# Gated linear attention and an MLP-mixer on one core: float32 warming products, constants from three engines, one relu per row tile of batch 0, and a new order for all engines

## The chip, the cores and the metric

The kernel runs on one core of a Trainium2 chip. The metric is the device time of one execution in microseconds (us); lower is better. Engines are named as the profile names them: PE (TensorE, matrix products), PEld (its weight loads), DVE (VectorE), ACT (ScalarE), POOL (GpSimd) and SP (SyncE, which only issues transfers here). A page of the profile shows one execution.

## The reference, cut to what matters

```python
# q, k, v, f_logit: (4, 8, 768, 48), float32
f = 1.0 / (1.0 + np.exp(-f_logit))
for t in range(S):                      # 768 steps, state (B, H, 48, 48)
    state = f[:, :, t, :, None] * state + np.einsum('bhd,bhe->bhde', k[:, :, t], v[:, :, t])
    y[:, :, t] = np.einsum('bhd,bhde->bhe', q[:, :, t], state)
x = y as (B, S, H * D)                  # (4, 768, 384)
xt = x.transpose(0, 2, 1)
h = np.maximum(xt @ w_tok1, 0.0) @ w_tok2       # (768 x 256), (256 x 768)
u = x + h.transpose(0, 2, 1)
h2 = np.maximum(u @ w_ch1, 0.0) @ w_ch2         # (384 x 1536), (1536 x 384)
return u + h2
```

## The kernel before, in words

Each of the four batches goes through two stages. The attention stage cuts the 768 steps into six chunks of 128. For a chunk it takes the logarithms of the gates (`exp`, `ln` on ACT), the low half of their split into two bf16 numbers (`lo`, a subtraction on DVE or POOL), their running sums as matrix products with a triangle of ones (`sums` on PE), the two factors `G` and `Gi` (exponentials on ACT), the gated q and k (`gated`, DVE), their transposes (`turn` on PE, `turned` the copy out of PSUM), the scores within the chunk (`scores`, PE), their causal mask (`masked`, DVE), and the result `y` from scores and v and from the carried state. The state is carried by `tsum` (state plus k'v, DVE), `state` (times the chunk's decay, DVE), and two `spread` copies into the bf16 operand `state_bd` of the next chunk's `y`. Batch 0 handles its chunks in three pairs, and there `within` is the product of masked scores and v for both chunks, and `parts` the k'v products. `x_bf` and `x_nat` are copies of `y` in bf16 and in float32.

The mixer stage of a batch is `tok1` (12 products of 384 columns into two row tiles), `h1T` (the relu of each row tile), `tok2` (12 products), `u` and `u_bf` (the sums with x), `ut`/`uT` (transposes), `ch1` (24 tiles of three products), `zT` (their relus), `ch2` (six tiles of twelve products), the last sum and the store. In batch 0 each `h1T` row tile is relued in two halves of 192 columns.

Nothing is scheduled by a program at run time. Each engine runs its queue in order and waits at semaphores. The order is the string `ORDER`: each number is one operation in the order in which the code made it, a letter behind it names the engine (A, D or G for ACT, DVE or POOL) where it can choose, and numbers behind colons are PSUM banks. A token z or s is a run of products whose result is not used, 512 or 64 columns wide, on a tile of ones (`steady`, made by a DVE memset); they keep PE at work where it would wait. POOL also issues nearly all loads, each holding its queue for about 0.9 us; loads rotate over eight semaphores, so that one waits for the landing of the load eight places ahead of it. The loads of f for batch 0 and all stores go through SP.

Constants (zeros around the 48 used columns of 64, the triangle `tri`, the identity, pair masks `pmask0`, `pmask1`, `inc2`, `exc2`) are made once, by DVE except for `tri`, which POOL makes from a tile that DVE has zeroed. `L870` is the line of the idle products, `L698` the masks of batch 0, `L536` those of the others, `L730` and `L549` the state's decay, `L352` and `L354` the relus on ACT and DVE.

## Time and profile before

| | |
|---|---|
| median of three timed runs | 173.82 us (173.77 to 174.5) |
| profiled execution, first to last instruction | 172.8 us |
| PE busy, share of the span | 95%, clock 0.999 of full |
| DVE, ACT, POOL busy | 75%, 64%, 45% |
| queue of POOL's loads | 13.77 MB, 91.7% of the span on 16 DMA engines |

The profiled execution has no time of its own beside its span. The median of the runs lies 1.0 us above that span; that is what is around the first and last instruction. A busy share of PE says little on how full it is, since products overlap in the records; how close together they start says more, and so does the chain of waits.

### The profile page before, as it was taken

The numbers are of one execution on the slowest core, as the hardware profiler recorded it, in microseconds if no ns is written. First come the engines' busy times: TensorE is split into PE (matmuls) and PEld (weight loads), VectorE is DVE, ScalarE is ACT, GpSimd is POOL, SyncE is SP. The second block draws the span as 40 slices with busy tenths as digits, with TensorE's granted clock in tenths as the row PEclk, the third lists the DMA queues.
The fourth block names the chain that finished last, engine by engine and source line by source line (L and its number), as shares of the span: only waits on it lengthen the run. The fifth ranks groups of instructions, "written<-read, shape, count | busy, mean of one in ns | idle before, by whom it ended". The sixth has DMA issues, their size and how long they took to land.

```text
span 172.8 us, 4455 instructions
## 1 busy us (share of the span) xinstructions
PE 164.4 (95%) x1758; PEld 103.6 (60%) x1762; DVE 129.1 (75%) x287; ACT 109.7 (64%) x246; POOL 78.0 (45%) x102
## 2 busy tenths in 40 slices
PE   6889998999999999999999999999999999999991
PEld 2465755566676666676667566666565656656660
DVE  6989996978997789989969859887786355581132
ACT  3997938999893656799999685479933430444100
POOL 2999846998566893799663330010101012000000
PEclk9999999999999999999999999999999999999999
DMA  5999999999997998999999995638155006250054
GB/s 146 217 169 175 246 210 210 157 122 129 197 134 154 182 109 197 133 60 114 108 135 69 63 141 135 144 81 157 32 154 154 1 19 163 89 188 0 2 200 168
DMA packets 89573, 22.74 MB, mean 132 GB/s; under 512 B 82288, under 2 KB 88736, under 8 KB 89552
## 3 DMA queue, kind: packets, MB, share of 16 engines
q0 software_dynamic: 69600, 13.77, 91.7%
q1 hardware_dynamic: 19952, 8.69, 19.6%
q8 instruction: 14, 0.23, 0.6%
q14 instruction: 7, 0.06, 0.1%
HBM read 25.17 MB, written 4.72 MB: 173 GB/s over the span
## 4 chain that ended last, share of the span: by engine, by line
PE 75%; ACT 8%; DVE 5%; issue 1%; DVEq 0%
PE ps L838 26%; PE ps L819 23%; PE ps L750 4%; PE ps L766 4%; PE ps L408 3%; ACT zT L352 2%; PE ps L495 2%; PE ps L456 2%; PE ps L560 2%; PE ps L457 1%; ACT L L367 1%; PE ps L870 1%; PE ps L424 1%; PE ps L804 1%; PE ps L556 1%
## 5 line engine op out<-in xcount | busy, mean ns | idle before, releaser
L838 PE MATMUL ps<-w_ch,zT 128*128 128x384 bf16 (+2 forms) x300 | 52.9, 319 | 0.0
L819 PE MATMUL ps<-uT,w_ch 128*128 128x384 bf16 x288 | 52.4, 326 | 0.3 <-ACT GG L468 0.2
L352 ACT ACTIVATE zT<-ps 128x384 bf16<-128x384 f32 x61 | 28.2, 493 | 19.6 <-PE ps L819 14.6
L838 PEld LDWEIGHTS <-zT 128*128 128x128 bf16 x300 | 28.4, 98 | 17.4 <-issue 0.2
L819 PEld LDWEIGHTS <-w_ch 128*128 128x128 bf16 x288 | 26.9, 97 | 17.0 <-issue 0.7
L354 DVE TENSOR_SCALAR zT<-ps 128x384 bf16<-128x384 f32 x35 | 18.9, 554 | 10.4 <-PE ps L819 8.9
L536 DVE TENSOR_TENSOR AmT<-ps,tri_bf 128x512 bf16<-128x512 f32 x36 | 23.1, 683 | 2.3 <-PE ps L408 2.1
L348 POOL CAST state_bd<-state 48x192 bf16<-48x192 f32 x24 | 9.0, 376 | 34.6 <-DVE state L549 22.2
L844 DVE TENSOR_TENSOR x_nat<-x_nat,ps 128x384 f32<-128x384 f32 (+2 forms) x25 | 12.8, 534 | 10.3 <-PE ps L838 9.8
L264 POOL DMA_DIRECT2D qk_sb<-in_q_dram x16 | 15.9, 1000 | 0.8 <-issue 0.8
L264 POOL DMA_DIRECT2D qk_sb<-in_k_dram x16 | 15.7, 983 | 0.3 <-issue 0.3
L264 POOL DMA_DIRECT2D v_sb<-in_v_dram x16 | 15.7, 983 | 0.1
L782 DVE TENSOR_TENSOR x_nat<-x_nat,ps 128x384 f32<-128x384 f32 x21 | 10.8, 549 | 4.2 <-PE ps L766 4.1
L750 PE MATMUL ps<-x_bf,w_tok 128*128 128x384 bf16 x48 | 13.2, 326 | 0.3 <-DVE zT L698 0.2
L348 POOL CAST u_bf<-x_nat 128x384 bf16<-128x384 f32 x6 | 3.0, 506 | 20.7 <-DVE x_nat L782 20.7
L374 POOL TENSOR_TENSOR Llo<-L 128x384 bf16<-128x384 f32 x10 | 8.2, 826 | 6.4 <-ACT L L367 6.3
L485 DVE TENSOR_TENSOR qk<-qk_sb,GG 128x768 bf16<-128x768 bf16 x18 | 9.9, 555 | 1.4 <-ACT GG L468 1.4
L870 PE MATMUL ps<-x_nat 128*128 128x512 bf16 x26 | 8.7, 460 | 2.0 <-DVE x_nat L279 1.5
L466 ACT ACTIVATE GG<-ps 128x384 bf16<-128x384 f32 x18 | 8.7, 492 | 2.5 <-PE ps L457 2.3
L344 ACT ACTIVATE x_bf<-ps 128x384 bf16<-128x384 f32 x13 | 6.5, 499 | 5.9 <-PE ps L560 5.0
L766 PE MATMUL ps<-h1T,w_tok 128*128 128x384 bf16 x48 | 9.4, 326 | 0.8 <-ACT h1T L352 0.6
L468 ACT ACTIVATE GG<-ps 128x384 bf16<-128x384 f32 x18 | 8.9, 492 | 1.8 <-PE ps L457 1.6
(96 smaller groups left out, 266.4 us busy)
## 6 DMA issues: line engine op xcount, KB each, us to landing
out_dram<-x_nat SPq DMA_DIRECT2D x23, 192.0 KB, 2.2
f_sb<-in_f_logit_dram POOLq DMA_DIRECT2D x3, 1152.0 KB, 11.1
f_sb<-in_f_logit_dram SPq DMA_DIRECT2D x3, 384.0 KB, 4.2
w_ch<-in_moe_w_ch_dram POOLq DMA_DIRECT2D x2, 576.0 KB, 13.2
qk_sb<-in_q_dram POOLq DMA_DIRECT2D x12, 96.0 KB, 6.6
qk_sb<-in_k_dram POOLq DMA_DIRECT2D x12, 96.0 KB, 5.6
v_sb<-in_v_dram POOLq DMA_DIRECT2D x12, 96.0 KB, 4.5
w_ch<-in_moe_w_ch_dram POOLq DMA_DIRECT2D x1, 1152.0 KB, 10.0
```

The source lines that it names most:

```text
L264: lambda eng=eng, into=into, of=of: eng.dma_start(out=into, in_=of),
L348: nc.gpsimd.tensor_copy(out_, in_)
L352: nc.scalar.activation(out_, in_, AF.Relu, bias=0.0, scale=1.0)
L354: nc.vector.tensor_scalar(out_, in_, 0.0, None, ALU.max)
L536: add(("masked", b, c, p), DVE, lambda half=half, made=made: nc.vector.tensor_tensor(half, made(), tb4, ALU.mult), need=["tri_bf"], make=[ ...
L750: add(("tok1", b, rt, kt), PE, lambda rt=rt, kt=kt, pm=pm: nc.tensor.matmul(banks[pm.at][:, 0:DM], lhsT=w_tok1[:, kt, rt * 128:(rt + 1) * ...
L766: nc.tensor.matmul(banks[pm.at][:, 0:DM], lhsT=w_tok2[:, kt, tt * 128:(tt + 1) * 128], rhs=h1T[:, kt, :], start=(kt == 0 and not held), st ...
L782: nc.vector.tensor_tensor(to, un, banks[pm.at][:, 0:DM], ALU.add)
L819: nc.tensor.matmul(banks[pm.at][:, 0:384].rearrange("p (n t) -> p n t", t=128), lhsT=w[:, kt, c0:c0 + 128], rhs=uT[:, rows3, kt, :], start ...
L838: nc.tensor.matmul(banks[pm.at][:, 0:n1 - n0], lhsT=zT[:, kt, tt * 128:(tt + 1) * 128], rhs=w_ch2[:, kt, n0:n1], start=(kt == 0), stop=(kt ...
L844: add(("sum", b, tt, n0), DVE, lambda un=un, pm=pm, n=n1 - n0: nc.vector.tensor_tensor(un, un, banks[pm.at][:, 0:n], ALU.add), make=[("x_n ...
L870: nc.tensor.matmul(banks[NBANK - 1][0:rows, 0:cols], lhsT=steady[:, 0:rows], rhs=steady[:, 0:cols], start=True, stop=True)
```

## The change

Five things are changed at once.

- Idle products: the tokens z and s of before (13 of 512 columns at the start, then 17 more up to the end of batch 0's attention) give way to tokens w: one float32 product of the given number of columns on the same tile of ones, read as float32. There are three of 512 columns and eleven bf16 products of 64 columns at the start, and one of 512 and one of 128 columns ahead of the second `within`.
- Constants: memsets may stand on DVE or POOL, copies on DVE or ACT. The new list puts eleven memsets on POOL and five copies on ACT.
- State: the decay product may stand on POOL; twelve of its sixteen products from the second chunk on do so, three of them in batch 0.
- `h1T` of batch 0 is relued in whole rows of 384 columns: two operations in place of four.
- `ORDER` is a new list: order, engines and banks of all operations. Counts by engine that change most: `zT` on ACT 61 to 55, on DVE 35 to 41; `lo` on POOL 11 to 15, on DVE 13 to 9; `u_bf` on ACT 14 to 11, on POOL 6 to 10; `turned` on ACT 8 to 5, on DVE 10 to 13; `uT` on ACT 5 to 2, on DVE 7 to 10; `x_bf` and `x_nat` on ACT 25 to 29, on DVE 20 to 16.

```diff
+HALVES = False
+STATES = (DVE, POOL,)
 ORDER = """
-32 33 10 5 34 15 21 9 8 22 13 11 0 1 36 24 27 2 49 3 6 35 12 14 20 23 25 26 50 28 7 37 51 52D 54 53D 38 17 z13 105:0
+w512 w512 w512 s11 32 0G 6G 33 8G 20D 9D 5G 34 13D 7G 1 21G 35 2 24A 23A 27D 3A 37 26A 29D 14D 28 49 17D 36 19D 51 22G
...
     def memset(name, tl, value, make, own):
-        once(name, DVE, lambda: nc.vector.memset(tl, value), make, own)
+        op = once(name, (DVE, POOL), None, make, own)
+        op.fn = lambda: (nc.gpsimd if op.engine == POOL else nc.vector).memset(tl, value)
+
+    def copied(name, out_, in_, make, own, need):
+        op = once(name, (DVE, ACT), None, make, own, need)
+        op.fn = lambda: copy_on(op.engine, out_, in_)
...
-                add(("state", b, c), DVE, lambda: nc.vector.tensor_tensor(state, tsum, gb, ALU.mult),
-                    need=["tsum", ("glast", g4)], make=["state"], kind=small)
+                decayed(b, c, gb, ("glast", g4))
...
+    def decayed(b, c, gb, key):
+        op = add(("state", b, c), STATES, None, need=["tsum", key], make=["state"], kind=("el", HP * D, True, 1))
+        op.fn = lambda: (nc.gpsimd if op.engine == POOL else nc.vector).tensor_tensor(state, tsum, gb, ALU.mult)
...
-            half = DM // 2 if b == 0 else DM
+            half = DM // 2 if b == 0 and HALVES else DM
...
     def idle(n, cols):
+        if not cols:
+            wide = spare[:, 0:512].bitcast(FP32)
+            nc.tensor.matmul(banks[NBANK - 1].rearrange("p (a n) -> p a n", n=128)[:, 0:n // 128], lhsT=wide[:, 0:128],
+                             rhs=wide[:, 0:128].unsqueeze(1).broadcast_to((128, n // 128, 128)), start=True, stop=True)
+            return
```

**PE, around the second `within`.** Before, PE's queue holds one last product of `within` (L711), then six idle products (one is shown), then the past-state product of chunk 2 (L736):

```order
L711 LDWEIGHTS zT
L711 MATMUL ps_114<-v_sb_72,zT 128x48
L870 LDWEIGHTS x_nat_101
L870 MATMUL ps_119<-x_nat_101 128x512
L736 LDWEIGHTS zT
L736 MATMUL ps_112<-state_bd_98,zT 128x96
```

With the change the two float32 idle products stand ahead of `within` (now L719), behind the last scores (L676):

```order
L676 LDWEIGHTS zT
L676 MATMUL ps_114<-zT 64x128
L877 MATMUL ps_119<-x_nat_101 128x512
L877 MATMUL ps_119<-x_nat_101 128x128
L719 LDWEIGHTS zT
L719 MATMUL ps_116<-v_sb_72,zT 128x48
```

Nothing idle is left between `within` and the products with the state.

**DVE, at the end of batch 0's attention.** Before, from the last mask on (L698; `x_bf` is L346, the halves of `h1T` L354):

```order
L698 TENSOR_TENSOR zT<-ps_117,x_nat_101 128x512
L728 TENSOR_TENSOR tsum<-state,ps_116 128x192
L730 TENSOR_TENSOR state<-tsum,gpair_120 128x192
L346 CAST x_bf_102<-ps_114 128x384
L346 CAST x_bf_102<-ps_117 128x384
L346 CAST x_bf_102<-ps_113 128x384
L354 TENSOR_SCALAR h1T<-ps_115 128x192
L354 TENSOR_SCALAR h1T<-ps_118 128x192
L346 COPY x_nat_99<-ps_112 128x384
```

With the change (masks are L706, `tsum` L736, `state` L577, copies L279, `h1T` L359):

```order
L706 TENSOR_TENSOR zT<-ps_115,x_nat_101 128x512
L736 TENSOR_TENSOR tsum<-state,ps_114 128x192
L577 TENSOR_TENSOR state<-tsum,gpair_120 128x192
L279 CAST x_bf_102<-ps_116 128x384
L279 CAST x_bf_102<-ps_117 128x384
L279 CAST x_bf_102<-ps_113 128x384
L359 TENSOR_SCALAR h1T<-ps_114 128x384
L279 COPY x_nat_99<-ps_116 128x384
```

One whole row of `h1T` stands in the place of two halves; the other row is one ACT operation.

**POOL, in the second half of batch 0's attention.** Before, from the second token weights on (`spread` is L348, loads of q, k, v L264, of weights L270):

```order
L270 DMA w_tok_65<-in_moe_w_tok_dram 128x2x768 [waits DMASW3_49]
L348 CAST state_bd_98<-state 48x4x48
L270 DMA w_ch_67<-in_moe_w_ch_dram 128x3x768 [waits DMASW4_49]
L270 DMA w_ch_66<-in_moe_w_ch_dram 128x3x768 [waits DMASW5_49]
L348 CAST state_bd_97<-state 48x4x48 [waits DVE_49,PE_49]
L264 DMA qk_sb_70<-in_q_dram 128x8x48 [waits DMASW6_49]
```

With the change (`state` is L577, `spread` L281, loads L266 and L272, `lo` L379):

```order
L272 DMA w_tok_65<-in_moe_w_tok_dram 128x2x768 [waits DMASW3_49]
L577 TENSOR_TENSOR state<-tsum,gpair_120 128x192 [waits DVE_49,Activation_49]
L266 DMA qk_sb_70<-in_q_dram 128x8x48 [waits DMASW4_49]
L266 DMA qk_sb_70<-in_k_dram 128x8x48 [waits DMASW5_49]
L272 DMA w_ch_67<-in_moe_w_ch_dram 128x3x768 [waits DMASW6_49]
L281 CAST state_bd_98<-state 48x4x48 [waits Pool_49]
L577 TENSOR_TENSOR state<-tsum,gpair_121 128x192 [waits DVE_49,Activation_49,Pool_49]
L266 DMA qk_sb_70<-in_k_dram 128x8x48 [waits DMASW7_49]
L281 CAST state_bd_97<-state 48x4x48 [waits PE_49,Pool_49]
L266 DMA qk_sb_70<-in_q_dram 128x8x48 [waits DMASW0_49]
L272 DMA w_ch_66<-in_moe_w_ch_dram 128x3x768 [waits DMASW1_49]
L577 TENSOR_TENSOR state<-tsum,gpair_121 128x192 [waits DVE_49,Activation_49,Pool_49]
```

The state's products now stand in the queue that issues the loads, behind loads that wait for landings of earlier ones.

119 lines of the change are left out of this document (58 added, 61 removed).

## The prediction

> **What bounds the kernel now.** I read the page's first part and the table of windows, then the chain of waits, then the timeline of the first 34 us and the groups by line.
>
> ```profile
> span 172.8 us, 4455 instructions
> 10.00:20.00 10.00, 8.91 (x219) 6.22 (x218) 9.58 (x27) 8.14 (x19) 9.01 (x12) 1.00 1.81 196
> 20.00:30.00 10.00, 8.92 (x185) 5.58 (x180) 8.09 (x16) 6.62 (x16) 6.03 (x10) 1.00 1.10 213
> 33.90:51.80 17.90, 17.80 (x201) 11.69 (x201) 16.29 (x34) 16.87 (x41) 13.90 (x18) 1.00 1.97 145
> 72.60:105.10 32.50, 32.22 (x357) 21.24 (x355) 26.78 (x56) 28.15 (x65) 19.10 (x21) 1.00 1.69 105
> 145.76 10.72 PE ps L819 x66
> ```
>
> A window's row gives its length, then busy us of PE, PEld, DVE, ACT, POOL, and the granted clock. The last row is a piece of the chain: 66 products in 10.72 us, 0.162 us each, PE without a gap. From 138 us to the last product the chain is such pieces, so the end is moved only by what happens earlier. From 33.9 to 105 us DVE and ACT are nearly as full as PE (16.29 and 16.87 of 17.9 us), and PE sometimes waits for them. From 10 to 20 us DVE is the full one (9.58 of 10 us); PE is then kept going by idle products. The first 34 us are the costly part: the chain there runs so:
>
> ```profile
> 24.68 1.24 PE ps L870 x5
> 26.73 0.51 PE ps L711 x32
> 29.21 0.37 DVE h1T L354
> 29.61 0.56 ACT h1T L352 x2
> 30.19 0.37 DVE h1T L354
> 30.60 1.46 PE ps L766 x8
> 33.19 0.34 PE ps L804 x6
> 33.88 0.26 PE ps L819
> 47.47 0.45 PE ps L495 x8
> 82.60 0.51 ACT zT L352
> ```
>
> At 24.68 us PE runs its own idle products (1.24 us) while the state's product, `parts` and the other `within` stand behind them. At 29.21 us four half relus follow one another before `tok2` (L766) can go on at 30.60. At 33.88 the chain reaches the channel products (L819), whose first stands at 33.81. A transpose takes 0.056 us (L804 and L495, 6 and 8 of them). At 82.60 the chain lies on ACT.
>
> **The change part by part.** *The start.* These rows carry it:
>
> ```profile
> 1.46 4.72 PE L870 MATMUL ps<-x_nat 128*128 128x512 bf16 x13 [1.46 <-DVE x_nat L279]
> 3.32 0.29 POOL L282 TENSOR_SCALAR_AFFINE_SELECT tri_bf<-tri_bf 128x128 bf16<-128x128 bf16 x1 [2.88 <-DVE tri_bf L277]
> 5.94 0.96 DVE L396 TENSOR_TENSOR Llo<-L 128x384 bf16<-128x384 f32 x2
> 8.33 1.00 ACT L622 ACTIVATE GG<-ps 128x384 bf16<-128x384 f32 x2
> 9.88 1.17 DVE L629 TENSOR_TENSOR qk<-qk_sb,GG 128x384 bf16<-128x384 bf16 x4 [0.64 <-DMA qk_sb<-in_k_dram]
> 24.07 1.88 DVE L698 TENSOR_TENSOR zT<-ps,x_nat 128x512 bf16<-128x512 f32 x3
> 27.26 1.54 DVE L346 CAST x_bf<-ps 128x384 bf16<-128x384 f32 x3
> L277 DVE MEMSET L<- 128x256 f32 x3 | 0.8, 272 | 0.0
> L348 POOL CAST state_bd<-state 48x192 bf16<-48x192 f32 x24 | 9.0, 376 | 34.6 <-DVE state L549 22.2 <-DVE state L544 6.1 <-PE ps L736 3.1
> L549 DVE TENSOR_TENSOR state<-tsum,glast 128x192 f32<-128x192 f32 x12 | 4.2, 351 | 0.8 <-ACT state_bd L344 0.6 <-POOL state_bd L348 0.2
> L346 DVE COPY qkT<-ps 128x1024 bf16<-128x1024 bf16 x9 | 6.2, 686 | 0.4 <-PE ps L495 0.4
> L383 ACT ACTIVATE L<-f_sb 128x768 f32<-128x768 f32 x2 | 1.7, 854 | 0.0
> ```
>
> POOL waited 2.88 us for DVE's zeros; now it makes them, and four larger memsets, itself. No row shows a POOL memset of that size: between DVE's 0.27 and POOL's cast of 192 columns scaled to 256 (0.376 x 256/192 = 0.5), the four take 1.1 to 2.0 us, and the triangle is there between 2.0 us and 3.3 us; I take 2.8, nearer the cast, and the first load then issues 0.6 us earlier. That load is now k's, not q's, so the 0.64 us that DVE waited for k at 9.88 go. `Gi` of the first pair still starts at 8.33, since ACT has the same exponentials and logarithms before it; the list puts the earlier-needed one first. DVE's gated products can start at about 8.9 instead of 9.88.
>
> From there to the last mask (24.07 + 1.88 = 25.95 us) DVE's work hardly changes: three states go (3 x 0.35) and two small constants (about 0.6); a `lo` (0.48), an `x_bf` (0.51) and a `turned` (0.69) come: about zero. But ACT now has a logarithm of 0.85 us ahead of the second `Gi` and two more `spread` copies, and DVE waits for it about 1 us in all at the second and fourth gated products and at chunk 5's. I keep the last mask at 25.9. Gain so far 0, bounds -0.5 and +1.
>
> *The idle products.* The 1.24 us at 24.68 are gone from behind `within`. What is late next is the last mask: the second `within`, at 26.73 before, can run at 26.0, and `tsum`, which waited for `parts` behind those idle products, runs right behind the mask. The new idle products stand ahead of the first of the two `within`, whose masks end near 24.4, and the scores end near 22: no trace shows a float32 product; between the price of a bf16 one (1.24/5 = 0.25 us for 512 columns) and four times that the two take 0.3 to 1.2 us, inside that wait. At the start three of them take 1.1 us (at 4.72/13 = 0.36 us each) to 4.4 us; the `sums` wait for `lo` until 6.7 us (6.9 before, 5.94 + 0.96), so neither end delays them.
>
> *The end of batch 0's attention.* Last mask 25.9; `tsum` and `state` 0.7 us: 26.6; `spread` 0.36 on two engines: 27.0; chunk 5's `y` behind chunk 4's, one `sums` and three `tok1`: 27.5 to 27.8; its `x_bf` 0.51: 28.3, against 28.8 before (27.26 + 1.54). Row 0's relu on DVE (0.5, priced like that cast) runs beside the last three `tok1` of row 1; row 1's on ACT (0.5, as the `Gi` above) ends at 29.6 to 29.8. `tok2` gets both rows then; before, at 30.60. The first channel product follows from the same `u`, `ut`, `uT` steps at 33.0 instead of 33.81: 0.8 us. By then PE has also done one more chunk's `sums` (two products, 0.32), eight transposes of batch 1 (0.45) and one more `ut` (0.17), all placed where it waited: 0.95 us less to do later. The lead is 1.75 us; I take 1.6, bounds 0 (masks late) and 2.2.
>
> *The rest.* Rows for what changes engine:
>
> ```profile
> L374 POOL TENSOR_TENSOR Llo<-L 128x384 bf16<-128x384 f32 x10 | 8.2, 826 | 6.4 <-ACT L L367 6.3
> L374 DVE TENSOR_TENSOR Llo<-L 128x384 bf16<-128x384 f32 x8 | 4.4, 561 | 0.0
> L352 ACT ACTIVATE zT<-ps 128x384 bf16<-128x384 f32 x61 | 28.2, 493 | 19.6 <-PE ps L819 14.6 <-issue 4.3 <-ACT grow L472 0.2
> L344 ACT ACTIVATE u_bf<-x_nat 128x384 bf16<-128x384 f32 x12 | 6.1, 522 | 6.0 <-DVE x_nat L782 6.0
> L344 ACT ACTIVATE qkT<-ps 128x1024 bf16<-128x1024 bf16 x3 | 3.1, 1022 | 0.0
> ```
>
> From the first channel product on, DVE loses nine states (3.2 us), five `lo` (2.8) and five copies of `y` (2.6) and gains six `zT` (3.1, priced like those copies) and two `turned` (1.4): -4.1 us (three `uT` come, and some single operations of that size go). ACT loses six `zT` (3.0), five `u_bf` (2.6), two `turned` (2.0), two `uT` (1.0, priced like `zT`) and five gate operations now done earlier (2.5), and gains five copies of `y` (2.5) and two logarithm steps (1.0): about -8 us. POOL takes nine states, six `lo` (5.0) and four `u_bf` (2.0) and has four loads fewer. A POOL state is priced by the two `lo` rows: 0.351 x 826/561 = 0.52 us; bounds 0.35 and 0.83. So 12 us leave the two engines that crowd PE; in the two later windows quoted they were busy 88 us together. What PE then waits for is partly not load but order, which the new list also draws anew: I take a gain of 0.5 us, bounds -1.5 and +2.
>
> One row speaks against the moves: beside POOL's subtraction a small DVE copy took 0.78 us, without it 0.20.
>
> ```profile
> 9.04 0.20 DVE L323 COPY x_nat<-x_nat 64x64 bf16<-64x64 bf16 x1
> 10.97 0.83 POOL L396 TENSOR_TENSOR Llo<-L 128x384 bf16<-128x384 f32 x1 [0.23 <-ACT L L383]
> 11.07 0.78 DVE L323 COPY x_nat<-x_nat 64x64 bf16<-64x64 bf16 x1
> ```
>
> The Trainium skill, Advanced Engine Details and Errata, Mode Summary, says the same: the second SBUF port of the Vector engine is shared with GPSIMD, and two-port Vector instructions and GPSIMD instructions block each other. By that rule every such DVE instruction beside the new POOL work would stretch, and the sum would lose its 0.5 us. I keep the term: one instruction is no rate, and copies within SBUF are few after the start.
>
> The sum is made against the profiled execution: 172.8 - 1.6 - 0.5 = 170.7 us, and the 1.0 us by which the runs' median lies above its span: **171.7 us**.
>
> **The rivals.** *POOL's queue holds the state back (slower).* The place is the third state of batch 0 on POOL. It stands behind two loads that wait for the landings of f of batch 1 and of v's last piece, which follows f:
>
> ```profile
> f_sb<-in_f_logit_dram POOLq DMA_DIRECT2D x1, 1152.0 KB, 11.3
> w_tok<-in_moe_w_tok_dram POOLq DMA_DIRECT2D x1, 384.0 KB, 6.8
> 13.99 2.23 POOL L264 DMA_DIRECT2D f_sb<-in_f_logit_dram  x1
> 13.18 0.83 POOL L270 DMA_DIRECT2D w_tok<-in_moe_w_tok_dram  x1
> ```
>
> The weights landed at 20.0 (13.18 + 6.8), f at 25.3 (13.99 + 11.3), so f's 1152 KB took 5.3 us. The new list puts f ahead of those 384 KB and of 192 KB of v, 2.6 us at that rate, and starts 0.6 us earlier: an estimate of 22 us. v follows near 23, the weights' issue takes 0.8, and the state is made near 24.4; `tsum` wants it at 25.9. It decides when f lands after 23.5. At 25.3 the state comes at 27.7 and `lo` of batch 1's first chunk at 28.5; the `sums` that need it stand ahead of all `tok1` on PE, so `tok2` goes on 0.8 us later than now and not 0.8 earlier, and later states wait in the same queue: 173.8 + 0.8 to 1.5, some 174.9 us. Against it: the loads start earlier. Chance 0.17.
>
> *The lead is lost again (no change).* DVE and ACT still fill the channel stage; if PE waits for them, a head start of 1.6 us is given back there, as it is where the chain lies on ACT at 82.60: 173.4 us. Against it: 12 us less work on both. Chance 0.17.
>
> *The clock falls (slower).* Between 10 and 30 us the clock was 1.00 with 16 idle products of 512 columns there; now there are 640 columns. PE was busy 17.8 us in those 20, about 4 of them (16 x 0.25) idle products; a third of the other 13.8 us at half the rate costs 4.6 us, of which about half lies beside DVE's masks: 2.5 us on top of the forecast, 174.2. Against it: PE's longest wait in my walk is 1.3 us. Chance 0.06. The Trainium skill, TensorE: Matmul & The Clock Gate, PE-mode transpose, says that transposes do not count as busy for the clock gate; this stretch is rich in them. No run here shows whether it is so.
>
> **How the numbers follow.** Runs of this kernel spread by 0.4%, so 0.5% (0.87 us) is about what can be told from no change. Forecast (faster) 0.60; no change 0.17; slower 0.17 + 0.06 = 0.23. The forecast's own range is 169.7 (the rest's gain at its bound of 2.0 and the lead near its own) to 172.9 (where it meets no change). The 8-in-10 range takes in the rivals up to 174.9, where the POOL case mostly ends: 169.7 to 174.9.
>
> **What would show it.** Right: the first gated product before 9.3 us; no idle product on the chain near 24 us; both relus of `h1T` done before 30.0; the first channel product at 33.2 or earlier; ACT's pieces in the chain from 34 to 105 us fewer. Wrong: the last mask of batch 0 later than 26.5; POOL's third state after 25 us; a granted clock below 1.00 after 6 us; `sums` of batch 1 waiting for `lo` on POOL; or the lead there at 33 us and gone at 105 us.

## The result and the profile after

The changed kernel takes 173.26 us (median of 20 runs) where the kernel before takes 174.41 us; the ratio is 0.9927, 95% interval 0.9905 to 0.995. It is faster, by 0.7%. Medians are over all executions of a kernel; ratios and intervals leave out the slow ones, more than 1.5% above its fastest. The prediction said 171.7 us, 2.1 us below its own base of 173.82 and 2.7 us below the 174.41 of these runs. The direction came, but only 1.15 us of the size. The profiled execution has a span of 171.7 us and a time of 173.47 us, so 1.8 us lie around the span. The runs of the kernel before show the same 1.8 us (span 172.8 us, time 174.6 us).

The page of the changed kernel, its first line and the shares of the chain that ended last:

```profile
span 171.7 us, 4436 instructions
PE 74%; POOL 11%; DMA 7%; ACT 3%; issue 2%; DVE 1%; POOLq 0%; DVEq 0%
```

The same shares in the kernel before:

```profile
PE 75%; ACT 8%; DVE 5%; issue 1%; DVEq 0%
```

POOL holds 11% of that chain; the kernel before has none of POOL there. A window of the changed kernel, in the columns of the prediction, and the same in the kernel before:

```profile
60.00:66.00 6.00, 4.92 (x50) 3.08 (x48) 2.80 (x5) 1.05 (x3) 5.76 (x10) 1.00 2.02 123
```

```profile
60.00:66.00 6.00, 5.90 (x66) 3.75 (x59) 5.12 (x10) 3.88 (x9) 5.34 (x6) 1.00 1.82 103
```

The stretch from 60 to 66 us is where to look: PE is busy 4.92 of 6 us (5.90 before), while DVE and ACT, the engines that crowd PE in the prediction, are nearly idle (2.80 and 1.05) and POOL is full (5.76).

The first 34 us of the changed kernel in its chain of waits (start, length, what):

```profile
10.28 11.87 DMA f_sb<-in_f_logit_dram
...
24.29 0.52 POOL state L577
27.67 0.33 PE ps L743 x4
29.50 0.49 ACT h1T L357
30.01 0.48 ACT grow L477
30.51 0.49 ACT GG L471
31.00 0.38 ACT GG L473
31.38 0.41 ACT u_bf L277
```

And in its timeline (start, length, engine, operation, in brackets the idle time before it and what ended that):

```profile
1.98 0.29 POOL L297 TENSOR_SCALAR_AFFINE_SELECT tri_bf<-tri_bf 128x128 bf16<-128x128 bf16 x1
2.26 1.07 POOL L266 DMA_DIRECT2D qk_sb<-in_k_dram  x1
8.90 0.36 DVE L637 TENSOR_TENSOR qk<-qk_sb,GG 128x384 bf16<-128x384 bf16 x1 [0.28 <-ACT GG L630]
21.11 3.67 DVE L706 TENSOR_TENSOR zT<-ps,x_nat 128x512 bf16<-128x512 f32 x6
26.11 0.48 DVE L577 TENSOR_TENSOR state<-tsum,gpair 128x192 f32<-128x192 f32 x1 [0.92 <-ACT state_bd L277]
22.66 0.88 POOL L266 DMA_DIRECT2D qk_sb<-in_q_dram  x1 [2.30 <-DMA f_sb<-in_f_logit_dram]
1.46 5.38 PE L877 MATMUL ps<-x_nat 128*128 128x512 f32 x6 [1.46 <-DVE x_nat L294]
21.59 1.35 PE L877 MATMUL ps<-x_nat 128*128 128x512 f32 x4
```

The masks of batch 0 end at 24.78 us (21.11 + 3.67), over a us earlier than before. But a load of q on POOL waited 2.30 us for f's landing, and the third state stood behind it until 24.29 and was made at 24.81; DVE's next state then waited for its spreads. The first channel product starts at 33.60 us, against 33.81 before. From 43 to 66 us the same timeline reads, for POOL and then for two waits of PE:

```profile
43.68 2.27 POOL L266 DMA_DIRECT2D f_sb<-in_f_logit_dram  x1
57.91 0.88 POOL L266 DMA_DIRECT2D v_sb<-in_v_dram  x1 [1.74 <-DMA f_sb<-in_f_logit_dram]
...
59.64 1.78 POOL L266 DMA_DIRECT2D v_sb<-in_v_dram  x2
61.38 0.40 POOL L281 CAST state_bd<-state 48x192 bf16<-48x192 f32 x1
...
62.53 0.92 POOL L266 DMA_DIRECT2D v_sb<-in_v_dram  x1
63.52 0.50 POOL L577 TENSOR_TENSOR state<-tsum,glast 128x192 f32<-128x192 f32 x1
65.78 1.61 POOL L379 TENSOR_TENSOR Llo<-L 128x384 bf16<-128x384 f32 x2
61.83 0.33 PE L560 MATMUL ps<-state_bd,qkT 128*128 128x96 bf16 x4 [0.68 <-POOL state_bd L281]
64.87 0.33 PE L560 MATMUL ps<-state_bd,qkT 128*128 128x96 bf16 x4 [0.39 <-POOL state_bd L281]
```

The load at 57.91 is the eighth behind f of batch 2 and waits for f's landing (57.63). Six loads follow one another at 0.88 us each, and a spread, a state and two `lo` stand between and behind them. In the kernel before, f of batch 2 went out 6.9 us later and landed at 61.63; the eighth load behind it came only at 62.45 and did not wait:

```profile
50.55 2.23 POOL L264 DMA_DIRECT2D f_sb<-in_f_logit_dram  x1
62.45 2.24 POOL L264 DMA_DIRECT2D f_sb<-in_f_logit_dram  x1
```

To see where a lead is won and lost, I add up PE's work over the trace's rows: each product that is not idle counts the distance to the next one, at most what a product of its columns takes without a wait (0.162 us for 384 columns); the rest of the distance is loss. The prices are those of the full clock, so a stretch at a lower clock counts as loss too. All kernels do 146.3 us of it.

| kernel | first channel product | work by 35 us | by 60 | by 75 | by 140 | loss 60 to 75 |
|---|---|---|---|---|---|---|
| before | 33.81 | 18.7 | 42.0 | 56.6 | 117.4 | 0.4 |
| changed | 33.60 | 19.8 | 43.4 | 56.6 | 118.3 | 1.8 |
| changed, second profile (e0) | 33.66 | 19.8 | 43.4 | 57.0 | 118.8 | 1.3 |
| e1 batch 1's loads moved | 33.11 | 20.3 | 43.9 | 56.6 | 118.3 | 2.4 |
| e2 batch 2's loads moved | 33.67 | 19.8 | 43.4 | 54.1 | 115.8 | 4.2 |
| e3 both | 32.66 | 20.8 | 44.4 | 56.3 | 118.0 | 3.1 |
| e4 states on DVE | 33.46 | 19.9 | 43.5 | 57.5 | 118.8 | 1.0 |
| e5 loads behind lo | 33.35 | 20.1 | 43.7 | 55.0 | 116.4 | 4.0 |
| e6 before, new idle products | 33.99 | 18.4 | 41.8 | 56.4 | 117.2 | 0.4 |
| e7 bf16 idle products | 35.12 | 18.2 | 41.9 | 56.1 | 118.0 | 0.7 |
| e8 halves of h1T | 35.06 | 18.3 | 42.1 | 56.6 | 118.4 | 0.6 |
| e9 constants on DVE | 34.33 | 19.1 | 41.9 | 56.3 | 118.0 | 0.7 |
| e10 POOL freed at 58 us | 33.07 | 20.3 | 44.1 | 58.5 | 120.3 | 0.5 |
| e11 f of batch 2 by SP | 35.19 | 18.4 | 42.3 | 56.6 | 118.3 | 0.8 |
| e12 POOL freed, e1 left out | 34.06 | 19.3 | 43.1 | 57.5 | 119.3 | 0.4 |
| e13 only states and spreads off | 33.22 | 20.1 | 43.9 | 58.4 | 120.1 | 0.5 |
| e14 as e10, constants on DVE | 33.80 | 19.3 | 42.3 | 56.8 | 118.5 | 0.6 |
| e15 as e10, bf16 idle products | 35.20 | 18.2 | 42.1 | 56.5 | 118.3 | 0.6 |

The changed kernel leads by 1.1 us at 35 us and by 1.4 at 60; at 75 the lead is nil (0.4 in the second profile). The 0.9 us that it leads by at 140 were won after 75 us. One row is one execution: in the profiles of e7, e11, e12 and e15 the clock fell before 35 us, in those of e2 and e5 between 68 and 75.5 us.

### The profile page after: what moved, and what is told of

Same layout as the page of the kernel before. It is cut to its first block, busy times and chain, and to the rows that moved or that the text cites. A ratio compares the mean times of both kernels' runs of the same rounds, so it can differ in the third digit from the quotient of the medians.

```text
span 171.7 us, 4436 instructions
## 1 busy us (share of the span) xinstructions
PE 162.2 (94%) x1753; PEld 103.2 (60%) x1753; DVE 123.3 (72%) x262; ACT 105.9 (62%) x240; POOL 90.8 (53%) x131
## 3 DMA queue, kind: packets, MB, share of 16 engines
q1 hardware_dynamic: 19952, 8.69, 19.1%
## 4 chain that ended last, share of the span: by engine, by line
PE 74%; POOL 11%; DMA 7%; ACT 3%; issue 2%; DVE 1%; POOLq 0%; DVEq 0%
PE ps L826 27%; PE ps L845 24%; DMA f_sb<-in_f_logit_dram 7%; PE ps L757 4%; PE ps L773 4%; POOL qk_sb L266 4%; PE ps L500 3%; PE ps L413 3%; POOL v_sb L266 2%; PE ps L564 2%; PE ps L429 2%; PE ps L461 2%; PE ps L462 2%; PE ps L560 1%; PE ps L811 1%
## 5 line engine op out<-in xcount | busy, mean ns | idle before, releaser
L357 ACT ACTIVATE zT<-ps 128x384 bf16<-128x384 f32 x55 | 25.2, 491 | 21.5 <-PE ps L826 21.1
L826 PEld LDWEIGHTS <-w_ch 128*128 128x128 bf16 x288 | 26.8, 97 | 16.3
L359 DVE TENSOR_SCALAR zT<-ps 128x384 bf16<-128x384 f32 x41 | 21.4, 552 | 13.0 <-PE ps L826 12.6
L379 POOL TENSOR_TENSOR Llo<-L 128x384 bf16<-128x384 f32 x15 | 12.4, 834 | 11.8 <-ACT L L372 11.7
L266 POOL DMA_DIRECT2D qk_sb<-in_q_dram x16 | 15.7, 986 | 2.9 <-DMA f_sb<-in_f_logit_dram 2.3
L266 POOL DMA_DIRECT2D v_sb<-in_v_dram x16 | 15.8, 990 | 2.7 <-DMA f_sb<-in_f_logit_dram 1.7
L266 POOL DMA_DIRECT2D qk_sb<-in_k_dram x16 | 15.8, 990 | 0.0
L281 POOL CAST u_bf<-x_nat 128x384 bf16<-128x384 f32 x10 | 5.0, 508 | 14.6 <-issue 10.1
L281 POOL CAST state_bd<-state 48x192 bf16<-48x192 f32 x22 | 8.0, 363 | 8.0 <-PE ps L560 3.0
L757 PE MATMUL ps<-x_bf,w_tok 128*128 128x384 bf16 x48 | 11.9, 326 | 0.0
L577 POOL TENSOR_TENSOR state<-tsum,glast 128x192 f32<-128x192 f32 x9 | 4.6, 507 | 10.4 <-PE ps L826 4.9
L471 ACT ACTIVATE GG<-ps 128x384 bf16<-128x384 f32 x18 | 8.9, 492 | 1.9 <-PE ps L462 1.0
L371 ACT ACTIVATE f_sb<-f_sb 128x384 f32<-128x384 f32 x18 | 9.1, 524 | 1.3 <-DMA f_sb<-in_f_logit_dram 1.2
L372 ACT ACTIVATE L<-f_sb 128x384 f32<-128x384 f32 x18 | 9.5, 526 | 0.2
```

The costliest lines, as they stand in the source:

```text
L266: lambda eng=eng, into=into, of=of: eng.dma_start(out=into, in_=of),
L281: nc.gpsimd.tensor_copy(out_, in_)
L357: nc.scalar.activation(out_, in_, AF.Relu, bias=0.0, scale=1.0)
L359: nc.vector.tensor_scalar(out_, in_, 0.0, None, ALU.max)
L379: op.fn = lambda: (nc.vector if op.engine == DVE else nc.gpsimd).tensor_tensor(lo, full, hi, ALU.subtract)
L757: add(("tok1", b, rt, kt), PE, lambda rt=rt, kt=kt, pm=pm: nc.tensor.matmul(banks[pm.at][:, 0:DM], lhsT=w_tok1[:, kt, rt * 128:(rt + 1) * ...
```

## The experiments

Ratios are to the kernel before, run on the same chip, with 95% intervals.

**e1, the loads of batch 1 moved.** POOL's queue:

```diff
+L577 TENSOR_TENSOR state<-tsum,gpair_121 128x192
 L266 DMA qk_sb_70<-in_q_dram 128x8x48
 L272 DMA w_ch_66<-in_moe_w_ch_dram 128x3x768
-L577 TENSOR_TENSOR state<-tsum,gpair_121 128x192
 L379 TENSOR_TENSOR Llo<-L_78 128x8x48 x2
-L266 DMA v_sb_73<-in_v_dram 128x8x48
 L281 CAST state_bd_97<-state 48x4x48
-L266 DMA v_sb_73<-in_v_dram 128x8x48
+L266 DMA v_sb_73<-in_v_dram 128x8x48 x2
```

> The changed kernel with three loads of batch 1 moved back on POOL: q's second piece and half of w_ch1 behind the third state of batch 0, v's second piece behind the spread of the next state. Nothing else moves. Theory A (POOL's queue): in the changed kernel q's issue waited 2.30 us for the landing of f and the state stood behind it until 24.29 us. Without that the state is made near 21.6, the spread of it on ACT near 24.3 (behind the gate of batch 1), DVE's next state near 25.5 instead of 26.11, chunk 5's y near 26.9 instead of 27.67, the first channel product near 32.9 instead of 33.60: 0.5 to 0.8 us less, ratio to the kernel before 0.988 to 0.990 against 0.9927. Theory B (the queue costs nothing, ACT's gate of batch 1 sets the time there): first channel product within 0.2 us of 33.60, ratio 0.992 to 0.994. Theory C (a head start at 33 us is given back in the channel stage): first channel product near 32.9, yet ratio 0.992 to 0.994.

Measured 172.92 us, ratio 0.9934 (0.9909 to 0.9959). POOL's timeline of this kernel:

```profile
21.47 0.51 POOL L577 TENSOR_TENSOR state<-tsum,gpair 128x192 f32<-128x192 f32 x1 [0.75 <-DVE tsum L736]
```

The state comes at 21.5 us and the first channel product at 33.11: theory A's mechanism and its half us. The lead is 0.5 us larger at 60 us and gone at 75: for the time, theory C.

**e2, the loads of batch 2 moved.** POOL's queue:

```diff
+L281 CAST state_bd_98<-state 48x4x48
+L577 TENSOR_TENSOR state<-tsum,glast_90 128x192
+L281 CAST state_bd_97<-state 48x4x48 x2
 L266 DMA v_sb_74<-in_v_dram 128x8x48
 L266 DMA qk_sb_71<-in_k_dram 128x8x48
 L266 DMA v_sb_74<-in_v_dram 128x8x48 x2
-L281 CAST state_bd_98<-state 48x4x48
 L266 DMA qk_sb_71<-in_k_dram 128x8x48
 L266 DMA v_sb_74<-in_v_dram 128x8x48
-L577 TENSOR_TENSOR state<-tsum,glast_90 128x192
-L281 CAST state_bd_97<-state 48x4x48 x2
```

> The changed kernel with six loads of batch 2 (v, k, v, v, k, v, issued from 57.9 us on) moved back on POOL behind the spread of chunk 3's state, the state of chunk 4 and its two spreads. Nothing else moves. In the changed kernel PE lost 1.41 us between 60 and 65 us, in the kernel before 0.38; a spread ran at 61.38 and the state at 63.52, both behind loads, the first of which waited 1.74 us for f's landing. Theory A (POOL's queue): the state is made near 60.2, PE loses 0.4 us or less there, and 0.7 to 1.0 us goes from the whole: ratio 0.987 to 0.989 against 0.9927. Theory B (PE would have waited there for something else, the masks on DVE at 61.7 us): PE loses 1.0 us or more there still, ratio 0.992 to 0.994. Theory C (given back later): PE loses 0.4 us there, and the ratio is 0.991 or more.

Measured 176.53 us, ratio 1.0126 (1.0069 to 1.0184): slower, which no theory had. From PE's timeline in this kernel, and from its windows (the clock is third from the end):

```profile
68.56 0.48 PE L462 MATMUL ps<-Llo,tri_bf 128*128 128x384 bf16 x1 [2.53 <-POOL Llo L379]
```

```profile
68.00:70.00 2.00, 1.44 (x5) 0.69 (x5) 0.00 (x0) 0.93 (x3) 2.00 (x3) 0.55 1.89 99
70.00:72.00 2.00, 2.00 (x9) 0.93 (x8) 0.92 (x2) 0.73 (x2) 0.55 (x2) 0.60 0.94 49
```

From 60 to 65 us PE loses nothing, as theory A had it. But the loads now stand ahead of `lo` of batch 2, PE waits 2.53 us for that instead, and behind the wait the clock is 0.55 to 0.60 for some 3.5 us, which is part of the 4.2 us of loss. Five of its six executions ran at a mean clock of 0.99 or less. Moving loads in a full queue only changed who waits.

**e3, both moves**, the two diffs above together.

> Both moves of loads on POOL together. Theory A (POOL's queue, the two losses add): 1.2 to 1.8 us less than the changed kernel, 171.5 to 172.1 us where the changed kernel has 173.3; ratio 0.983 to 0.986. Theory B (neither counts): ratio 0.992 to 0.994. Theory C (a lead is given back in the channel stage, so that only the loss at 60 us counts): ratio 0.987 to 0.989, as with the later loads moved alone.

Measured 175.6 us, ratio 1.0056 (1.0022 to 1.009). The first channel product is the earliest of all, 32.66 us, and PE loses 3.1 us from 60 to 75; nine of its twelve executions ran at a mean clock of 0.99. None of the theories held.

**e4, the states back on DVE.**

```diff
-163G
+163
-170G
+170
...
-451G
+451
```

> The changed kernel with all twelve states that it makes on POOL made on DVE instead, at the same places of the list. The spreads that POOL does and its loads stay. It undoes the move of the states alone. Theory A (POOL's queue): the third state of batch 0 comes near 21.6 as without the loads ahead, so the first channel product comes near 32.9 to 33.2; at 60 us a spread on POOL still stands behind the loads until 61.4, so about half of that loss stays; DVE gets 12 x 0.36 = 4.3 us more work, which costs some tenths: ratio 0.988 to 0.992. Theory B (the states on POOL are a gain, as the prediction's third term has it): DVE's 4.3 us more work delay PE by 0.5 us or more, ratio 0.995 or more.

Measured 173.76 us, ratio 0.9972 (0.994 to 1.0004): the median is worse than the changed kernel's, though the intervals overlap. The profiled execution, at clock 0.999, is better than that (span 171.3 us): PE loses 1.0 us in place of 1.8 from 60 to 75, as theory A had it. But the third state is not early. On DVE it stands behind four masks and comes at 24.16 us (24.29 on POOL), and the first channel product, at 33.46, misses theory A's. The three executions at 0.999 took 173.07 to 173.36 us, as the changed kernel does, and 8 of 11 executions ran at a mean clock of 0.99 and took up to 175.5 us. From 75 to 140 us it does 61.3 us of work, the changed kernel 61.7. Where the clock fell in those executions their times don't tell; so the test doesn't settle what the states alone are worth.

**e5, the loads behind `lo` too.** POOL's queue, with e1's move kept:

```diff
+L281 CAST state_bd_98<-state 48x4x48
+L577 TENSOR_TENSOR state<-tsum,glast_90 128x192
+L281 CAST state_bd_97<-state 48x4x48 x2
+L379 TENSOR_TENSOR Llo<-L_77 128x8x48 x2
 L266 DMA v_sb_74<-in_v_dram 128x8x48
+L266 DMA qk_sb_71<-in_q_dram 128x8x48
 L266 DMA qk_sb_71<-in_k_dram 128x8x48
...
 L281 CAST u_bf<-x_nat_100 128x384
```

> The changed kernel with the batch 1 loads moved back as in the first of these runs, and eight loads of batch 2 (from 57.9 us on) moved on POOL behind the spread of chunk 3, the state of chunk 4, its two spreads and also the two lo of batch 2 that follow. With only the state moved ahead of the six loads, lo came at 67.69 us instead of 65.78, and PE lost 3.45 us between 65 and 70 instead. Theory A (POOL as a whole is the bound from 58 to 68 us, and what PE waits for there must stand ahead of the loads): lo near 61.5 us, PE loses 0.8 us or less from 60 to 70 us where the changed kernel lost 1.43; the lead of 0.45 us won at 27 us stays: span 170.0 to 170.6 us against 171.7, ratio 0.981 to 0.987. Theory B (another wait follows at once: the loads that were moved are wanted by the gated products and parts of batch 2): PE loses 1.0 us or more between 65 and 80, ratio 0.991 to 0.995.

Measured 173.65 us, ratio 0.9956 (0.9914 to 0.9999). Its chain of waits:

```profile
61.26 1.61 POOL Llo L379 x2
...
69.89 0.51 POOL u_bf L281
```

`lo` comes at 61.3 us and the loss moves to 69 to 72, to `u_bf`, POOL's next work behind eight loads. Not theory B's transfers, and not theory A's hope: POOL has more to do from 57.6 to 72 us than fits, in each of the orders tried. The 4.0 us of loss are not all POOL's: this execution took 175.6 us, and its clock fell to 0.50 from 72.0 to 75.4.

**e6, the kernel before with the new idle products.**

```diff
-z13
+w512 w512 w512 s11
...
-z6
+w512 w128
```

> The kernel before with the changed kernel's idle products alone: three float32 ones and eleven of 64 columns at the start instead of thirteen bf16 ones of 512, the seven later groups taken out, and two float32 ones ahead of the second-last within. Its list is otherwise untouched, with loads, constants, states and halves of h1T as before. Theory A (as the prediction had it: the last mask at 25.95 us stands right behind the idle products, so they were worth 0.7 us at most): first channel product 33.2 to 33.7 us against 33.81, ratio 0.996 to 0.999. Theory B (the idle products held up the bf16 work in full, 1.24 us): first channel product near 32.6, ratio 0.993. Theory C (they kept the clock up): a clock below 0.99 in the first 35 us, ratio above 1.003.

Measured 174.58 us, ratio 0.9976 (0.9944 to 1.0009), first channel product 33.99 us. No difference can be told: the interval allows a gain of up to 1 us, but the first channel product came no earlier than before (33.81), and not at theory A's 33.2 to 33.7.

**e7, the float32 idle products in bf16.**

```diff
-w512 w512 w512 s11
+z1 z1 z1 s11
...
-w512 w128
+z1
```

> The changed kernel with each idle float32 product of 512 columns replaced by one bf16 product of the same columns (the 128-column one is left out). The three at the start then end near 2.6 us instead of 6.8, and PE waits 4 us for the sums. In a run with a wait of 2.4 us at 66 us the clock was 0.55 to 0.60 for the 3.5 us behind it. Theory A (a long wait costs clock): the clock is below 0.8 in the first sums and turns, from 7 to 11 us, and the first channel product comes 0.5 to 1.5 us later than 33.60: ratio 0.996 to 1.002. Theory B (the clock does not matter while DVE is the full engine): first channel product within 0.2 us of 33.60, ratio 0.991 to 0.995.

Measured 174.0 us, ratio 0.9977 (0.9942 to 1.0011). Two `sums` of this kernel, the same two of the changed kernel, and windows of e7:

```profile
7.16 0.53 PE L618 MATMUL ps<-L,x_nat 128*128 128x384 bf16 x1
7.49 0.52 PE L618 MATMUL ps<-Llo,x_nat 128*128 128x384 bf16 x1
```

```profile
7.57 0.33 PE L618 MATMUL ps<-L,x_nat 128*128 128x384 bf16 x1
7.74 0.32 PE L618 MATMUL ps<-Llo,x_nat 128*128 128x384 bf16 x1
```

```profile
20.00:22.00 2.00, 1.09 (x40) 0.79 (x29) 1.67 (x3) 1.95 (x4) 1.46 (x3) 1.00 1.56 174
22.00:24.00 2.00, 1.33 (x47) 0.83 (x38) 2.00 (x5) 1.61 (x4) 0.89 (x2) 1.00 1.44 202
24.00:26.00 2.00, 1.21 (x34) 1.00 (x34) 2.00 (x4) 0.64 (x2) 1.98 (x4) 0.88 1.46 196
26.00:28.00 2.00, 1.92 (x55) 1.72 (x54) 0.89 (x4) 1.73 (x5) 1.70 (x3) 0.50 1.95 177
```

The clock is low twice. Behind the idle start, where theory A looked, the `sums` follow one another at 0.32 us up to about 11.7 us, where the changed kernel's follow at 0.16: half the clock. (The windows say 1.00 there, since the trace has no clock record before its first, at 11.86 us in e7.) The first gated product comes at 9.31, not 8.90. Then the clock falls again at 25.5 us, behind 6 us in which PE is busy 60% with no gap over 1.2 us. In the changed kernel the float32 pair at 21.59 us keeps PE busy for 1.35 us just there, and the clock stays at 1.00. Every execution of e7 had a mean clock of 0.976 to 0.99. The first channel product comes 1.5 us later, the time rises by 0.75. The edit takes both groups of float32 products away, so which of them the second fall hangs on is not separated.

**e9, the constants on DVE.**

```diff
-0G 6G
+0D 6D
...
-21G 24A 23A
+21D 24D 23D
```

> The changed kernel with all its constants made by DVE again (ten memsets that POOL makes and five small copies that ACT makes), at the same places of the list; POOL still makes the triangle. It undoes the sharing of the constants alone. Theory A (they gave the earlier start): the first gated product at 9.4 us or later instead of 8.90, DVE's masks of batch 0 end 0.5 to 1.2 us later than 24.78, the first channel product near 34.0 instead of 33.60; of that POOL's queue at 60 us takes a part: ratio 0.993 to 0.998. Theory B (the constants never stood on the path): first gated product within 0.2 us of 8.90, ratio 0.991 to 0.994.

Measured 174.03 us, ratio 0.9979 (0.9951 to 1.0008): theory A. DVE's first gated product, from its timeline:

```profile
10.22 0.36 DVE L637 TENSOR_TENSOR qk<-qk_sb,GG 128x384 bf16<-128x384 bf16 x1 [1.23 <-ACT GG L630]
```

It starts at 10.22 in place of 8.90 us, the first channel product at 34.33. The edit also puts the memset of `grow` into DVE's queue in the channel stage, and PE waits behind it:

```profile
34.87 0.48 DVE L288 MEMSET grow<- 32x512 f32 x1 [0.16 <-issue]
36.00 0.33 PE L811 MATMUL ps<-ident,u_bf 128*128 128x128 bf16 x3 [0.53 <-DVE x_nat L279]
```

So not all of the 0.8 us that this kernel takes longer than the changed one is the start.

**e0, e10, e11 and e8, on one chip.** e0 is the changed kernel, unedited.

> The changed kernel once more, unedited, as the measure for the three beside it. All theories: 172.6 to 173.6 us, ratio to the kernel before 0.990 to 0.995.

Measured 173.15 us, ratio 0.9915 (0.9886 to 0.9945). e10 has e1's move and takes six operations off POOL:

```diff
-427G 451G 452G 453G 589G 586G
+427A 451D 452A 453D 589D 586D
```

> The changed kernel with the batch 1 loads moved back as in the first run, and with six operations taken off POOL between 58 and 68 us: the state of batch 1's chunk 4, one spread and two lo of batch 2 go to DVE, two spreads to ACT, at the same places of the list. POOL then has nothing but loads to issue there, in the old order. Theory A (POOL's total from f's landing at 57.6 us on is the bound; neither order of loads helped, since eight issues of 0.88 us stay ahead of something): PE loses 0.5 us or less from 60 to 75 us where the changed kernel lost 1.82, the lead of 1.4 us over the kernel before at 60 us, and 0.45 more from the first move, stays: span 169.9 to 170.6 us, ratio 0.981 to 0.986. Theory B (PE is held there by DVE and ACT, which were idle only because POOL held PE): PE loses 1.2 us or more, ratio 0.990 to 0.995. Theory C (a lead over the kernel before is given back later, from 75 to 135 us): PE loses 0.5 us or less at 60 to 75, ratio 0.988 or more.

Measured 171.81 us, ratio 0.9825 (0.9782 to 0.9867): theory A, and faster than both kernels. Its four executions at full clock took 171.28 to 172.07 us, less than any of the changed kernel (172.62 at least); the two at a mean clock of 0.99 took 173.94 and 174.18. Its window, and then POOL's timeline:

```profile
60.00:66.00 6.00, 6.00 (x58) 3.91 (x57) 4.35 (x10) 2.31 (x7) 4.32 (x5) 1.00 2.45 142
```

```profile
57.32 0.88 POOL L266 DMA_DIRECT2D v_sb<-in_v_dram  x1 [1.66 <-DMA f_sb<-in_f_logit_dram]
...
67.30 0.50 POOL L281 CAST u_bf<-x_nat 128x384 bf16<-128x384 f32 x1 [2.98 <-DVE x_nat L789]
```

The loads stand as before and still wait for f, but nothing that PE wants stands behind them; POOL is idle for 2.98 us before `u_bf`, and PE is busy 6.00 of 6 us.

e11 has e1's move and takes f of batch 2 out of POOL's row of eight:

```diff
-            eng = nc.gpsimd if engine == POOL else nc.sync
+            eng = nc.gpsimd if engine == POOL and (n, b, cs.start) not in BY_SP else nc.sync
```

> The changed kernel with the batch 1 loads moved back as in the first run, and with f of batch 2 issued by SP, behind the glast of batch 1's chunk 3, instead of by POOL. POOL's loads wait in turn for the landing of the load eight issues before; f no longer stands in that row, and its issue of 2.2 us leaves POOL. Theory A (the ring of eight with f in it makes the backlog at 58 us): no load waits for f, v's piece that was issued at 57.91 goes by 55, the state of chunk 4 is made by 60.5, PE loses 0.6 us or less from 60 to 75; span 169.9 to 170.8 us, ratio 0.981 to 0.987. Theory B (the DMA engines are the bound, f lands no earlier and the others wait in the same backlog): f lands after 57.0 us, and the loads behind it land no earlier than in the changed kernel; PE loses 1.0 us or more, ratio 0.990 to 0.995.

Measured 173.0 us, ratio 0.9929 (0.9898 to 0.9959): no gain over e1, so theory A is not shown. f landed at 58.97 us, as theory B had it. The profiled execution can't say more on 60 us, since its clock fell at 19 us and it came late there:

```profile
18.00:20.00 2.00, 1.76 (x31) 1.29 (x32) 1.94 (x6) 1.08 (x3) 1.76 (x3) 0.75 1.02 215
20.00:22.00 2.00, 1.22 (x24) 0.95 (x22) 1.81 (x3) 1.59 (x4) 0.45 (x2) 0.50 1.58 177
```

It shows something else. The clock was about half from 19 to 26 us, the first channel product came at 35.19 us, 2.1 us later than in e1; at 75 us the work done is 56.6 us in both. The loss at 60 us swallows a late start as it swallows a lead.

e8 has `h1T` of batch 0 in halves again:

```diff
-HALVES = False
+HALVES = True
```

> The changed kernel with h1T of batch 0 in halves as in the kernel before: each row by one ACT and one DVE operation of 192 columns, one after the other. It undoes the whole rows alone. Theory A (as the prediction had it: row 0's relu runs beside the last products of row 1, and whole rows save one step of two): tok2 goes on 0.2 to 0.4 us later than 29.63 us, ratio 0.993 to 0.995. Theory B (the halves are quicker by the time of half an operation behind the last product): tok2 0.1 to 0.3 us earlier, ratio 0.990 to 0.993. Theory C (ACT's and DVE's other work there decides): within 0.1 us of it.

Measured 173.51 us, ratio 0.9951 (0.9921 to 0.998). The chain of this kernel:

```profile
28.17 0.33 PE ps L743 x4
...
30.23 0.38 ACT GG L473
30.61 0.23 ACT h1T L357
30.87 0.36 DVE h1T L359
```

The halves end at 31.23 us, the whole rows at 29.99. Of the 1.24 us between, 0.5 were there before (chunk 5's `y` starts at 28.17, not 27.67), and 0.38 are a `Gi` of batch 1 that stands between ACT's two halves, while DVE's last half waits for ACT's. What is left of it speaks for theory A. In the time it is 0.4 us against e0, but the intervals overlap, so the gain of the whole rows is likely and not shown.

**What was still open (e12 to e15).** e12 is e10 without e1's move:

```diff
-427G 451G 452G 453G 589G 586G
+427A 451D 452A 453D 589D 586D
```

> The changed kernel with the six operations taken off POOL between 58 and 68 us as before (state, one spread, two lo to DVE, two spreads to ACT), but with the loads of batch 1 left where the change put them. Theory A (the first move is worth its 0.5 us at the first channel product, and with POOL's cover at 60 us gone it reaches the end): span 170.1 to 170.6 us, 0.4 to 0.6 more than the run with both, ratio 0.984 to 0.988. Theory B (the window alone makes the gain): the same as with both, 169.5 to 169.9 us, ratio 0.982 to 0.984.

Measured 172.54 us, ratio 0.9884 (0.984 to 0.9928): near theory A. By the times, e1's move is worth 0.7 us with POOL freed and was worth 0.2 to 0.3 without; the intervals overlap in both cases. In the profiled execution the clock fell at 22.7 us, so its first channel product (34.06) says little; the other four, at full clock, took 172.42 to 172.79 us.

e13 is e10 with the two `lo` left on POOL:

```diff
-427G 451G 452G 453G
+427A 451D 452A 453D
```

> As the run with both moves, but only the state and the three spreads of batch 1 leave POOL between 58 and 68 us (state and one spread to DVE, two spreads to ACT); the two lo of batch 2 stay on POOL behind the loads. Theory A (the states and spreads, half of which the change brought to POOL, make the loss): PE loses 0.5 us or less from 60 to 70 us, span 169.8 to 170.3 us, ratio 0.982 to 0.987. Theory B (the lo hold as much, since they are POOL's and stand behind the same loads): lo near 65 us, PE loses 0.8 us or more between 65 and 72, span 170.8 us or more, ratio 0.988 or more.

Measured 171.84 us, ratio 0.9873 (0.9814 to 0.9932): theory A. Its interval overlaps that of e0, but its four executions at full clock took 171.53 to 171.86 us, less than any of the changed kernel. One state and three spreads, 0.50 + 3 x 0.36 us, make the loss; the two `lo` may stay.

e14 is e10 with e9's edit, e15 is e10 with e7's:

```diff
-0G 6G
+0D 6D
```

> As the run with both moves (loads of batch 1, six operations off POOL at 58 to 68 us), and all constants made by DVE as in the kernel before. In the changed kernel that cost 0.7 us at the first channel product. Theory A (a delay at the start counts in full once POOL does not hold PE at 60 us): span 170.4 to 170.8 us against 169.5 to 170.3, ratio 0.985 to 0.989. Theory B (another cover takes its place): within 0.3 us of the run with both, ratio 0.981 to 0.984.

```diff
-w512 w512 w512 s11
+z1 z1 z1 s11
```

> As the run with both moves, and the float32 idle products replaced by bf16 ones of the same 512 columns. In the changed kernel the clock then was 0.50 to 0.88 from 24 to 30 us, the first channel product came 1.5 us later, and the time rose by 0.75 us. Theory A (the float32 products hold the clock, and the whole loss counts once POOL does not hold PE at 60 us): first channel product at 34.3 us or later, clock 0.976 to 0.99, span 170.8 to 171.6 us, ratio 0.987 to 0.993. Theory B (with the batch 1 loads moved, PE waits less near 25 us and the clock holds): clock 0.995 or more, within 0.4 us of the run with both, ratio 0.981 to 0.985.

e14: 174.13 us, ratio 0.9985 (0.9954 to 1.0016), worse than theory A said: with POOL's loss gone, the constants count for 2.3 us (174.13 against 171.81), while at the changed kernel they counted for 0.8. The memset of `grow` has its part here as in e9: e14 is 1.0 us of work behind e10 at 35 us and 1.8 at 60. e15: 174.05 us, ratio 0.9963 (0.9933 to 0.9993): theory A's clock and its late first channel product (35.20 us), and 2.2 us in the time. All its executions ran at 0.98 to 0.99. One of its windows:

```profile
24.00:26.00 2.00, 2.00 (x55) 1.74 (x56) 1.31 (x3) 1.11 (x3) 1.99 (x3) 0.50 1.65 182
```

## Why the prediction was wrong in size

The direction came because most of the lead came: 1.1 us by 35 us, where 1.6 were forecast. The step that failed is the sum's other gain, "I take a gain of 0.5 us": DVE and ACT were relieved as it says, but what POOL's queue would do at 60 us stood in it at nothing, and there PE lost 1.8 us. As much was missing in the lead (0.5 us), and 0.8 us in the base. The parts follow.

**The start.** The first gated product came at 8.90 us, as predicted (8.9). The first load went out at 2.26 us, 1.3 us earlier than before where 0.6 were forecast, because the triangle came at 1.98, at the early bound of 2.0. Undoing the constants moved the gated product to 10.22: this step is shown.

**The last mask and the idle products.** "I keep the last mask at 25.9" was wrong: 24.78. The wait for ACT that was to eat the gain did not come. The idle float32 products cost more than their bounds said, 1.35 us for the pair and 5.38 us for three (upper bounds 1.2 and 4.4), four to five times bf16. The Trainium skill, FP8 and Floating Point Precision, TensorE Precision Notes, gives four passes through the array for true float32; 1.35 us against 0.31 for 640 bf16 columns at 24.68 us agrees. (The trace shows each float32 product as two records, so the three are x6 and the pair x4.) The pair was hidden behind the masks. At the start "neither end delays them" was not quite so: `lo` was done at 6.61 us, and the `sums` began at 7.23, right behind the idle products.

**The end of batch 0's attention.** `y` of chunk 5 at 27.67 (predicted 27.5 to 27.8) and the second relu done at 29.99 (29.6 to 29.8) fit nearly, but by two errors that cancel: the masks were early, and the third state on POOL was too late to use that. The estimates of f's landing, 22 us (22.15), and of the state, 24.4 (24.81), were near; that `tsum` wants it only at 25.9 was not, since the masks that set that ended early. With the state made at 22.0 (e1) the first channel product comes at 33.11. "The first channel product follows from the same `u`, `ut`, `uT` steps at 33.0" failed in a second way: from the last relu to that product 3.6 us went by, in the changed kernel and in e1, where the kernel before took 3.25. In both ACT puts `grow` and two gate exponentials of batch 1 (1.35 us) ahead of `u_bf`; no run moves these, so the cause of the 0.35 us stays open. The term of 1.6 us measured 1.1: 0.2 at the first channel product, where 0.8 were forecast, and 0.9 of other work done by then, as forecast (0.95).

**The rest.** "I take a gain of 0.5 us" measured about nothing (-0.05): +0.3 from 35 to 60 us, -1.4 from 60 to 75, +0.9 from 75 to 140, and small remainders. In e0's profile, with a span of 171.2 us, it measured +0.5, so the term scatters by half a us from one execution to another; the loss from 60 to 75 us stands in both (1.8 and 1.3 us, against 0.4 before). A state on POOL was priced rightly, 0.507 us on the page's group against 0.52. What was not priced is where it stands: behind loads that wait for f. The prediction saw that mechanism and wrote "later states wait in the same queue", but gave it a place at 25 us, a condition on f's first landing and a chance of 0.17; it did not ask the same of f's second landing. It also read the load of the engines only from 33.9 to 51.8 and from 72.6 to 105 us. The window between them, in the kernel before:

```profile
51.80:66.30 14.50, 14.40 (x156) 9.33 (x155) 11.74 (x25) 8.27 (x20) 11.85 (x14) 1.00 1.39 143
```

There ACT has room (8.27 of 14.5 us) and POOL, which the list loads further, is the fullest beside PE (11.85). At 25 us the queue cost 0.5 us at the first channel product (e1), at 60 us the whole lead (e10). The rival "the lead is lost again" came true as well, though not by DVE and ACT, which stood idle, but by POOL: the lead was there at 35 us and gone at 75. What was won afterwards is in part what the term counted on: by the rows of the two traces, PE's waits that ACT ended fall from 0.87 to 0.38 us between 75 and 140 us. Which part of the list brings the 0.9 us no run shows. The kernel before with the new idle products does not have it (60.8 us of work from 75 to 140, as in the unedited one), and every variant of the changed list has 61.3 us or more.

**The clock.** The rival is real, though it did not decide the result. Without the float32 products (e7, e15) the clock falls in every execution; with them it still falls in some. The mean clock was 0.99 or less in 11 of the changed kernel's 28 executions behind the two ratios (the result's and e0's), and in none of those of the kernel before. In e0 that cost nothing that can be told (172.96 to 173.91 us, against 173.06 to 173.20 in the others); in e10 the two executions at 0.99 took over 2 us longer. The busy share of PE alone does not decide it: e4's profiled execution kept 1.00 with PE busy 57% over 6 us (16.3 to 22.3). The Trainium skill, TensorE: Matmul & The Clock Gate, Part 1, gives two clocks, full and half; the 0.50 here agrees. The Trainium skill, TensorE: Matmul & The Clock Gate, Why this matters for your kernels, advises no PE gap over about 3 us; that is not enough in this case: in e11 the clock fell with no more than 0.8 us between the starts of products in the 8 us before.

**The base.** "The 1.0 us by which the runs' median lies above its span" joined one execution's span to the median of others. What lies around a span is 1.7 to 2.1 us in nearly every execution (1.8 in most); the same sum would have given 172.5. Against the profiled execution's 173.47 us the prediction was off by 1.8: 0.8 from this, 0.5 from the lead, 0.55 from the rest. The range, 169.7 to 174.9, held the time.

## What to carry to other kernels

In this kernel, work that others wait for did harm in a queue that issues loads, behind loads that wait for an earlier one's landing. Look for every such load, list what stands behind it, and ask that of each later turn of the loop, not of the first alone. A lead ahead of an engine that is full until a fixed event is mostly given back, and part of a delay is swallowed there: 1.5 us at the first channel product cost 0.4 us in e8 and 0.75 in e7. Test a change ahead of such a place again after it is cleared: the constants, with `grow` among them, counted for 0.8 us before and 2.3 after. Set a span against its own execution's time.

## What was not expected of the hardware

f of batch 2 landed between 56.9 and 57.7 us in all the variants of the changed list whose POOL issued it, at anything from 42.9 to 45.3 us. It landed 5.6 to 6.1 us behind the load of v just ahead of it, so the transfers queued ahead, more than the issue, seem to set it; no run moves those. The clock fell to half with no wait of PE over 1.2 us (e7, e11, e12, e15), where short gaps left it busy 45 to 60% for 2 to 6 us; but e4 kept it with 57% over 6 us. A POOL memset of 128x256 float32 took 0.28 us, as much as DVE's 0.27.
